# Sparse-and-full causal attention into a max-out FFN: V casts moved off VectorE, the opening reordered

## The chip, the cores and the metric

The kernel runs on one core of a Trainium2 chip. Five engines work side by side, each through its own queue in order: TensorE (matmuls and weight loads), VectorE (DVE in the profile), ScalarE (ACT), GpSimd (POOL) and SyncE (SP, which only issues DMAs here). An instruction that waits holds up all that stands behind it on its engine. The metric is the device time of one execution in microseconds, the median over runs.

## The reference

```python
def _attn_ref(q, k, v, is_retrieval, n_sink, window):      # B, H, S, D = 4, 8, 768, 64
    scores = scale * np.matmul(q, k.transpose(0, 1, 3, 2))
    stream_keep = causal & (is_sink | in_win)              # 4 sinks, a window of 64
    mask = causal if is_retrieval[head] else stream_keep
    a = softmax(where(mask, scores, -1e9))
    return np.matmul(a, v)

def _moe_ref(x, w1, w2, w3, w_out):                        # x: 3072 x 512, w: 512 x 768, w_out: 768 x 512
    h = np.maximum(np.maximum(x @ w1, x @ w2), x @ w3)
    return h @ w_out
```

Attention over 4 batches of 8 heads, where a flag of each head chooses between a full causal mask and a mask of sinks and a window; its result, heads side by side, goes through an FFN with a maximum over three products. All inputs are float32, the work is done in float16 with float32 accumulation.

## The kernel before

A *step* t is a batch, a half of its 768 queries, and four of its eight heads (`where`, L105): steps 0 to 3 are batch 0 (first half: 0 and 1, second half: 2 and 3), steps 4 to 7 batch 1, and so on to 15. The two head pairs of a step are i = 0 and 1. The scores of a step are cut into units u (`UNITS`, L19): two for a first half, four for a second one. For a unit, `scores` (L404) runs matmuls into PSUM (L439), ScalarE takes exp into an SBUF tile `pt` (L450), and `masks` (L460) multiplies blocks of `pt` by the head's mask (L477), on GpSimd unless the triple (t, i, u) stands in `MASK_ON_DVE`. For steps 0 and 1 the mask is added by matmuls instead (L423), so the scores need the mask tiles of `head_masks` (L291), which need the heads' flags (`head_flags`, L274).

`av` (L481) multiplies `pt` by V; V lies in two float16 copies, `va` for blocks near the diagonal and `vf`, multiplied by the head's flag, for far ones. `prep_v` (L384) makes both for a step and a head pair: a cast of the float32 load (L390) on the engine of its first letter, the product (L392) on that of its second. VectorE then takes a reciprocal and a product into x (L501, L503). x is transposed by a DMA, or by TensorE with an eviction (`turn_x`, L518) in steps 0, 1 and 3.

K and Q must stand transposed: in batch 0 they are loaded as float32, cast (`cast_pair`, L133), transposed on TensorE (L155) and evicted (L160, `turn_pair`); in batches 1 to 3 a casting DMA from GpSimd's queue (`load`, L169) is followed by four VectorE transposes for a step's heads (`turn`, L180: K or Q, first or second part). `stage` keeps three buffers of each load.

The FFN of a batch's half is a generator (`ffn`, L317) that yields 24 times: 18 groups of four 384-wide matmuls (L336) and three output blocks. A group of w1 is copied out by ScalarE (L344), those of w2 and w3 are combined by VectorE (L347). All single-bank PSUM tiles, those of FFN groups, V products and transposes, come from one pool of four banks (`bkp`); scores have two tiles of their own. `fill(n)` takes n yields off the queue of FFNs; an FFN enters this queue with `turn_x` of the last pair of its half.

The order is written out by hand: first an opening, line by line (L537 to L592), then `PROGRAM` (L600), one row for each score unit from step 2 on. I call a row a slot: slots 1 to 4 are step 2, 5 to 8 step 3, 9 and 10 step 4, 11 and 12 step 5. A row is (units of FFN to spend, whether the two pairs' scores stand apart, four strings of work: before the scores, after them, after half of the FFN units, after the rest). In the strings `v 2 0 dd` is `prep_v(2, 0)` with VectorE for both parts (a is ScalarE, p GpSimd), and `cast`, `pair`, `turn`, `load`, `load_v`, `av` and `x` name the functions above. `gate` lets SyncE's queue wait for step 3's first exps, so that its later V loads don't take part in the first loads.

The first weight w0 is loaded by `load_weight(0)` (L555) from GpSimd's queue, and so are the K and Q of batch 0's second half (`load_pairs(1, ...)`), the other weights, V of the second half, and all of `load`. `idle_work` (L223) runs matmuls of zeros, to no use but activity.

Of the kernel before, what the change touches and what calls it, by code (L numbers as in the profile page):

```python
# [33 lines left out]
MASKED = [  # L34
    [(0, 0, 1, (0,), 256, 256), (0, 0, 1, (384,), 128, 0), (1, 1, 1, (0,), 256, 0)],
    [(1, 0, 2, (384,), 128, 0), (2, 2, 1, (0, 384), 128, 128), (3, 3, 1, (0,), 256, 0)],
]


def _where(half):  # L40
# [9 lines left out]
def kernel(  # L50
# [14 lines left out]
    nc = tc.nc  # L65
# [50 lines left out]
    cast = {}  # L116
# [200 lines left out]
    def ffn(b, half):  # L317
# [10 lines left out]
        hT = [htp.tile([P, HALF], FP16, tag=f"hT{n}", name=f"hT{n}") for n in range(NNB)]  # L328
        acc = {}
        order = [(wi, ni) for ni in range(NNB) for wi in range(3)]  # L330
        if (b, half) == (0, 0):
            order.sort()
        for wi, ni in order:
            yy = psum()
# [120 lines left out]
                masks(t, i, u)  # L455


    MASK_ON_DVE = ((3, 1, 3), (6, 0, 1), (7, 0, 1))

    def masks(t, i, u):  # L460
        b, half, qd = where(t)
        pt = pts[t, i]
        h0 = 4 * qd + 2 * i
        for at, u0, nu, cols, n, m0 in MASKED[half]:
            if at != u:
                continue
            m = mk[:, h0 : h0 + 2, m0 : m0 + n]
            if nu == 1 and len(cols) == 1:
                x = pt[:, u0, :, cols[0] : cols[0] + n]
            elif nu == 2:  # L470
                x = pt[:, u0 : u0 + 2, :, cols[0] : cols[0] + n]
                m = m.unsqueeze(1).to_broadcast([P, 2, 2, n])
            else:
                x = pt[:, u0].rearrange("p h (c n) -> p h c n", n=n)[:, :, 0:4:3]
                m = m.unsqueeze(2).to_broadcast([P, 2, 2, n])
            engine = nc.vector if (t, i, u) in MASK_ON_DVE else nc.gpsimd
            engine.tensor_tensor(out=x, in0=x, in1=m, op=ALU.mult)  # L477
# [40 lines left out]
    def turn_x(t, i, op=None):  # L518
# [15 lines left out]


    dve, act, pool = nc.vector.tensor_copy, nc.scalar.copy, nc.gpsimd.tensor_copy
    idle_work(8)  # L537
    cast_pair(0, 0, (act, act))
    read_flags()
    head_flags()  # L540
    head_masks(0, True)
    turn_pair(0, 0, dve, dve)
    idle_work(2)
    cast_pair(0, 1, (pool, act))
    head_masks(1, True)
    turn_pair(0, 1, dve)
    cast_pair(0, 2, (pool, pool))
    scores(0, 0, (0,))
    turn_pair(0, 2, dve)
    scores(0, 0, (1,))  # L550
    head_masks(2, True)
    head_masks(3, True)
    cast_pair(0, 3, (pool, pool))
    scores(0, 1, (0,))
    load_weight(0)  # L555
    turn_pair(0, 3, dve)
    far_flags()
    prep_v(0, 0, dve, nc.gpsimd)
    scores(0, 1, (1,))
    prep_v(0, 1, dve, nc.vector)  # L560
    prep_v(1, 0, dve, nc.vector)
    scores(1, 0, (0,))
    scores(1, 1, (0,))
    prep_v(1, 1, dve, nc.gpsimd)
    load_pairs(1, 0, 2, (nc.gpsimd, nc.gpsimd))
    scores(1, 0, (1,))
    scores(1, 1, (1,))
    av(0, 0)
    load_weight(1)
    av(0, 1)  # L570
    load_pairs(1, 2, 2, (nc.gpsimd, nc.gpsimd))
    av(1, 0)
    turn_x(0, 0, act)
    turn_x(0, 1, act)
    av(1, 1)
    turn_x(1, 0, act)
    load_weight(2)
    load_v(0, 1, (nc.gpsimd,) * HB)
    load_weight(3)
    turn_x(1, 1, dve)  # L580
    cast_pair(1, 0, (dve, act))
    cast_pair(1, 1, (dve, act))
    fill(4)
    turn_pair(1, 0, dve)
    turn_pair(1, 1, dve)
    head_masks(0)
    head_masks(1)
    fill(1)
    head_masks(2)
    fill(1)  # L590
    fill(1)
    head_masks(3)  # L592

# [2 lines left out]

    FIRST = 4
    PROGRAM = (  # L600
        (2.4, True, "", "", "cast 1 2 dd", "cast 1 3 ap"),
        (2.4, False, "load 1 0", "", "", ""),
        (2.0, False, "pair 1 2", "", "", "pair 1 3"),
        (2.2, False, "load 1 1", "", "", ""),
        (2.2, True, "", "", "v 2 0 dd", "gate"),
        (1.6, True, "v 2 1 ap, load_v 1 0", "", "av 2 0", ""),
        (1.6, True, "", "x 2 0, turn 1 0 0 0, turn 1 0 0 1", "av 2 1, turn 1 0 1 1", "v 3 0 pp"),
        (3.0, False, "turn 1 0 1 0, load_v 1 1", "x 2 1", "", "v 3 1 ap"),
        (3.6, False, "", "turn 1 1 0 0, turn 1 1 0 1, turn 1 1 1 1, av 3 0", "", "v 4 0 pd"),
        (3.0, False, "av 3 1", "", "", "turn 1 1 1 0, v 4 1 ad"),  # L610
        (3.6, False, "x 3 0, x 3 1", "", "av 4 0", ""),
        (3.6, False, "", "v 5 0 ad, x 4 0, av 4 1", "", "v 5 1 ap, load 2 0"),
        (2.8, False, "", "x 4 1", "", ""),
        (3.6, False, "av 5 0, av 5 1, load 2 1", "x 5 0", "", ""),
        (3.8, False, "v 6 0 pp", "x 5 1", "", "load_v 2 0"),
        (3.4, False, "", "v 6 1 dp", "", "turn 2 0 1 0"),
        (4.8, False, "", "turn 2 0 0 1", "av 6 0", "turn 2 0 0 0"),
        (4.0, False, "", "", "x 6 0, turn 2 0 1 1", "x 6 1"),
        (3.4, False, "", "av 6 1", "turn 2 1 0 0, turn 2 1 0 1", "load_v 2 1"),
        (5.0, False, "", "v 7 0 dp", "turn 2 1 1 0, turn 2 1 1 1", ""),  # L620
        (4.0, False, "v 7 1 dp", "", "", "v 8 0 ap"),
        (3.6, False, "av 7 0, x 7 0, av 7 1", "", "", "v 8 1 dp"),
        (4.0, False, "", "v 9 0 dp", "av 8 0, x 7 1", ""),
        (4.0, False, "", "av 8 1", "x 8 0", "load 3 0"),
        (4.0, False, "", "x 8 1", "av 9 0, v 9 1 dp", ""),
        (4.0, False, "load 3 1", "", "x 9 0", ""),
        (4.2, False, "v 10 0 dp, av 9 1", "", "x 9 1", "load_v 3 0"),
        (4.0, False, "v 10 1 dp", "", "", "turn 3 0 1 0"),
        (4.0, False, "", "turn 3 0 0 1, av 10 0", "", "x 10 0, turn 3 0 0 0"),
        (4.0, False, "", "", "av 10 1, turn 3 0 1 1", ""),  # L630
        (4.4, False, "", "x 10 1", "turn 3 1 0 0, turn 3 1 0 1", "v 11 0 dp, load_v 3 1"),
        (3.2, False, "", "", "turn 3 1 1 0, turn 3 1 1 1", "v 11 1 dp"),
        (4.0, False, "", "", "av 11 0", "v 12 0 dp"),
        (4.2, False, "x 11 0, av 11 1", "", "", "v 12 1 dp"),
        (4.8, False, "", "v 13 0 dp, x 11 1", "av 12 0", ""),
        (4.0, False, "", "av 12 1", "x 12 0", ""),
        (3.2, False, "", "x 12 1", "av 13 0, v 13 1 dp", ""),
        (4.0, False, "", "", "x 13 0", ""),
        (4.0, False, "v 14 0 dp, av 13 1", "", "x 13 1", ""),
        (4.0, False, "v 14 1 dp", "", "", ""),  # L640
        (4.0, False, "", "av 14 0", "", "x 14 0"),
        (4.0, False, "", "", "av 14 1", ""),
        (4.0, False, "", "x 14 1", "", "v 15 0 pp"),
        (4.2, False, "", "", "", "v 15 1 dp"),
        (4.0, False, "", "", "av 15 0", ""),
        (4.0, False, "x 15 0, av 15 1", "", "", ""),
        (4.0, False, "", "x 15 1", "", ""),
    )
    ops = {"d": dve, "a": act, "p": pool}
    engines = {"d": nc.vector, "p": nc.gpsimd}  # L650
# [74 lines left out]
```

## Time and profile before

| | |
|---|---|
| median of 10 runs | 203.73 us (202.21 to 205.49) |
| the profiled execution | 204.06 us, span 202.0 us |
| TensorE busy | 191.4 us (95%) |
| VectorE busy | 130.2 us (64%) |
| ScalarE busy | 124.8 us (62%) |
| GpSimd busy | 125.8 us (62%) |
| V casts (L390) | VectorE 22, mean 636 ns; ScalarE 6, mean 522 ns; GpSimd 4, mean 530 ns |
| mask products (L477) | GpSimd 81, VectorE 3 |
| HBM read, written | 25.17 MB, 6.29 MB |

The span goes from the first to the last instruction of one profiled execution; the time of an execution has some 2 us more. Busy time is an average over stages that differ: what counts in a stage is the wait that ends last. Matmuls are pipelined and their ends are modelled, so busy TensorE isn't TensorE at its peak. In a row of a view, the bracket behind an instruction tells how long its engine stood idle before it and who ended that.

### The profile page before, as it was taken

How to read it: one execution, taken by the hardware profiler on the slowest of the kernel's cores; microseconds unless marked ns; L12 is line 12 of the kernel's file. 1: busy time of each engine (PE TensorE's matmuls, PEld its weight loads, DVE VectorE, ACT ScalarE, POOL GpSimd, SP SyncE). 2: the span in 40 equal slices, each digit the busy share in tenths (PEclk: the TensorE clock that was granted, in tenths of full speed). 3: DMA queues.
4: the chain of work that ended last, by engine and by line, in shares of the span. 5: the costliest groups of instructions: out<-in, count | busy, mean ns of one | idle time of the engine just before them, and what ended most of it. 6: DMA issues, size and time to landing. Idle time of an engine off the chain costs nothing.

```text
span 202.0 us, 5148 instructions
## 1 busy us (share of the span) xinstructions
PE 191.4 (95%) x2059; PEld 109.3 (54%) x2059; DVE 130.2 (64%) x260; ACT 124.8 (62%) x188; POOL 125.8 (62%) x151
## 2 busy tenths in 40 slices
PE   7897899996999999999999999999999999999992
PEld 2555455544556456565556466574565565655652
DVE  2996697889456757985565748986647244633540
ACT  4492797895477778565758596656586776323221
POOL 3669279789993933859987806798929636700000
PEclk9999999999699999999999999999999999999998
DMA  6999999998929991632449982713301230024004
GB/s 181 268 150 236 274 236 206 214 232 187 206 48 191 185 248 59 127 51 76 144 80 204 178 199 83 143 21 124 93 19 24 86 93 19 3 42 153 3 0 156
DMA packets 43245, 26.48 MB, mean 131 GB/s; under 512 B 33558, under 2 KB 38230, under 8 KB 43222
## 3 DMA queue, kind: packets, MB, share of 16 engines
q1 hardware_dynamic: 37206, 15.01, 32.3%
q0 software_dynamic: 4784, 10.23, 26.1%
q10 hardware_dynamic: 1232, 0.92, 1.4%
q8 instruction: 16, 0.26, 0.5%
q14 instruction: 7, 0.06, 0.1%
HBM read 25.17 MB, written 6.29 MB: 156 GB/s over the span
## 4 chain that ended last, share of the span: by engine, by line
PE 82%; DVE 8%; DMA 4%; ACT 3%; POOL 1%; issue 1%; DVEq 0%; ACTq 0%
PE yy L336 43%; PE yy L362 13%; PE st L439 10%; PE oacc L493 9%; PE yst L336 3%; DMA qs<-in_q_dram 3%; DVE KQ L188 2%; PE st L226 2%; DVE KQ L160 2%; DVE mk L293 1%; ACT pt L450 1%; DMA out_dram<-ot 1%; PE tr L155 1%; PE yst L362 1%; ACT ot L368 1%
## 5 line engine op out<-in xcount | busy, mean ns | idle before, releaser
L477 POOL TENSOR_TENSOR pt<-pt,mk 128x512 f16<-128x512 f16 (+1 forms) x81 | 86.6, 1093 | 32.5 <-ACT pt L450 32.4
L450 ACT ACTIVATE pt<-st 128x1024 f16<-128x1024 f32 (+3 forms) x99 | 83.1, 894 | 27.0 <-PE st L439 26.4
L347 DVE TENSOR_TENSOR acc<-yy,acc 128x384 f16<-128x384 f32 x45 | 25.0, 557 | 25.7 <-PE yy L336 17.7
L336 PE MATMUL yy<-xT,w0t 128*128 128x384 f16 x180 | 36.7, 330 | 0.1
L336 PE MATMUL yy<-xT,w1t 128*128 128x384 f16 x180 | 36.7, 328 | 0.0
L336 PE MATMUL yy<-xT,w2t 128*128 128x384 f16 x180 | 36.2, 327 | 0.0
L344 ACT CAST acc<-yy 128x384 f16<-128x384 f32 x45 | 21.3, 481 | 19.9 <-PE yy L336 14.9
L362 PE MATMUL yy<-woutt,hT 128*128 128x512 f16 (+1 forms) x138 | 32.3, 375 | 0.0
L439 PE MATMUL st<-KQ 32*128 32x384 f16 (+5 forms) x560 | 29.2, 283 | 1.1 <-DVE KQ L188 0.7
L347 DVE TENSOR_TENSOR hT<-yy,acc 128x384 f16<-128x384 f32 x45 | 25.1, 557 | 6.4 <-PE yy L336 3.2
L493 PEld LDWEIGHTS <-pt 128*128 128x128 f16 x672 | 24.1, 98 | 5.5 <-issue 1.5
L493 PE MATMUL oacc<-va,pt 128*128 128x65 f16 x352 | 24.9, 194 | 0.8 <-POOL pt L477 0.8
L188 DVE STREAM_TRANSPOSE KQ<-kq 128x384 f32<-128x384 f32 x24 | 25.2, 1137 | 0.2 <-DMA kq<-in_k_dram 0.2
L336 PEld LDWEIGHTS <-w0t 128*128 128x128 f16 x192 | 17.9, 98 | 12.5 <-issue 1.4
L336 PEld LDWEIGHTS <-w2t 128*128 128x128 f16 x192 | 17.7, 98 | 13.0 <-issue 1.9
L336 PEld LDWEIGHTS <-w1t 128*128 128x128 f16 x192 | 17.5, 98 | 12.5 <-issue 1.1
L439 PEld LDWEIGHTS <-KQ 32*128 32x128 f16 (+1 forms) x560 | 12.5, 94 | 19.6 <-issue 13.9
L368 ACT COPY ot<-yy 128x512 f32<-128x512 f32 x22 | 12.9, 588 | 14.8 <-PE yy L362 10.6
L362 PEld LDWEIGHTS <-hT 128*128 128x128 f16 x150 | 13.8, 98 | 15.1 <-DVE hT L347 1.0
L493 PE MATMUL oacc<-vf,pt 128*128 128x65 f16 x320 | 21.4, 193 | 0.2 <-DVE vf L392 0.2
L501 DVE RECIPROCAL rc<-oacc 128x6 f32<-128x6 f32 x32 | 6.2, 193 | 19.6 <-PE oacc L493 19.4
L503 DVE TENSOR_TENSOR x<-oacc,rc 128x384 f16<-128x384 f32 x32 | 17.8, 557 | 1.1
(71 smaller groups left out, 125.6 us busy)
## 6 DMA issues: line engine op xcount, KB each, us to landing
out_dram<-ot SPq DMA_DIRECT2D x23, 256.0 KB, 2.6
vs<-in_v_dram SPq DMA_DIRECT2D x21, 256.0 KB, 5.2
kq<-in_k_dram POOLq DMA_DIRECT2D x6, 384.0 KB, 8.0
kq<-in_q_dram POOLq DMA_DIRECT2D x6, 384.0 KB, 9.4
qs<-in_q_dram ACTq DMA_DIRECT2D x4, 192.0 KB, 4.2
ks<-in_k_dram SPq DMA_DIRECT2D x4, 192.0 KB, 4.0
w0t<-in_moe_w_dram POOLq DMA_DIRECT2D x1, 768.0 KB, 7.0
ks<-in_k_dram POOLq DMA_DIRECT2D x2, 384.0 KB, 7.1
```

The lines of the kernel that those rows point to most:

```text
L188: nc.vector.transpose(out=dst.rearrange("c (p j) -> c j p", j=n)[:, j0:j1], in_=src.rearrange("c (j i) -> c j i", i=R),)
L336: nc.tensor.matmul(yy[:, 0:HALF], w_t[wi][:, ks, ni * P : (ni + 1) * P], xT[b, half][ks].rearrange("p a t -> p (a t)"), start=(ks == 0), s ...
L344: nc.scalar.copy(out=acc[ni], in_=yy[:, 0:HALF])
L347: nc.vector.tensor_tensor(out=dst, in0=yy[:, 0:HALF], in1=acc[ni], op=ALU.max)
L362: nc.tensor.matmul(yo[:, 0:n], hT[ns][:, tb * P : (tb + 1) * P], woutt[:, ns, c : c + n], start=(ns == 0), stop=(ns == NNB - 1),)
L368: op(out=ot[:, c : c + n], in_=yo[:, 0:n])
L439: nc.tensor.matmul(sts[g // m][:, g % m, c0 : c0 + n * P], KQ[rows, 0, ki * P : (ki + 1) * P], KQ[rows, 1, t0 : t0 + n * P], start=(c0 == ...
L450: nc.scalar.activation(out=pts[t, i][:, u, h0 : h0 + m, 0:w], in_=st[:, :, 0:w], func=AF.Exp, scale=sc,)
L477: engine.tensor_tensor(out=x, in0=x, in1=m, op=ALU.mult)
L493: nc.tensor.matmul(o[:, qi, hl, 0 : D + 1], pt[:, u, hl, c : c + P], vv[:, 2 * hp + hl, ki, 0 : D + 1], start=(idx == 0), stop=(idx == len ...
L501: nc.vector.reciprocal(out=rc, in_=o[:, :, :, D])
L503: nc.vector.tensor_tensor(out=x, in0=o[:, :, :, 0:D], in1=rc.unsqueeze(3).to_broadcast([P, HB, 2, D]), op=ALU.mult,)
```

## The change

V casts of steps 2 to 15 are written with `a` or `p` in place of `d`: 21 on ScalarE, 7 on GpSimd, none on VectorE. In steps 0 and 1 one V cast goes to ScalarE, one to GpSimd. Three `vf` products (steps 4 and 5) go from VectorE to GpSimd. Seven more mask products stand on VectorE, where step 3's joint mask of two units is split in two (`APART`). In the opening the first Q is evicted by ScalarE, two filler matmuls are moved ahead of the flags, `load_weight(0)` ahead of the casts of the fourth pair, `load_pairs(1, 0, ...)` ahead of a V step, and all four casts of batch 0's first two second-half pairs are put on ScalarE. The FFN of batch 0's second half also takes its groups in the order of the weights. `PROGRAM` has the same 47 rows, with other units (166.58 in place of 169.8 in all) and places. Of its rows, those up to slot 14 are shown, and slots 20, 27 and 39 of the new one.

```diff
--- before.py
+++ after.py
@@ -35,6 +35,8 @@
     [(0, 0, 1, (0,), 256, 256), (0, 0, 1, (384,), 128, 0), (1, 1, 1, (0,), 256, 0)],
     [(1, 0, 2, (384,), 128, 0), (2, 2, 1, (0, 384), 128, 128), (3, 3, 1, (0,), 256, 0)],
 ]
+
+APART = [(0, 0, 1, (384,), 128, 0), (1, 1, 1, (384,), 128, 0)] + MASKED[1][1:]
 
 
 def _where(half):
@@ -328,7 +330,7 @@
         hT = [htp.tile([P, HALF], FP16, tag=f"hT{n}", name=f"hT{n}") for n in range(NNB)]
         acc = {}
         order = [(wi, ni) for ni in range(NNB) for wi in range(3)]
-        if (b, half) == (0, 0):
+        if b == 0:
             order.sort()
         for wi, ni in order:
             yy = psum()
@@ -455,13 +457,13 @@
                 masks(t, i, u)
 
 
-    MASK_ON_DVE = ((3, 1, 3), (6, 0, 1), (7, 0, 1))
+    MASK_ON_DVE = ((2, 0, 1), (3, 0, 0), (3, 0, 1), (3, 1, 3), (5, 0, 0), (5, 1, 0), (5, 1, 1), (7, 0, 1))
 
     def masks(t, i, u):
         b, half, qd = where(t)
         pt = pts[t, i]
         h0 = 4 * qd + 2 * i
-        for at, u0, nu, cols, n, m0 in MASKED[half]:
+        for at, u0, nu, cols, n, m0 in APART if t in (3,) else MASKED[half]:
             if at != u:
                 continue
             m = mk[:, h0 : h0 + 2, m0 : m0 + n]
@@ -534,62 +536,62 @@
 
 
     dve, act, pool = nc.vector.tensor_copy, nc.scalar.copy, nc.gpsimd.tensor_copy
+    cast_pair(0, 0, (act, act))
     idle_work(8)
-    cast_pair(0, 0, (act, act))
     read_flags()
+    idle_work(2)
     head_flags()
+    turn_pair(0, 0, dve, act)
     head_masks(0, True)
-    turn_pair(0, 0, dve, dve)
-    idle_work(2)
     cast_pair(0, 1, (pool, act))
-    head_masks(1, True)
     turn_pair(0, 1, dve)
     cast_pair(0, 2, (pool, pool))
     scores(0, 0, (0,))
+    scores(0, 1, (0,))
+    head_masks(1, True)
+    load_weight(0)
+    scores(0, 0, (1,))
+    far_flags()
+    cast_pair(0, 3, (pool, pool))
+    head_masks(3, True)
+    head_masks(2, True)
     turn_pair(0, 2, dve)
-    scores(0, 0, (1,))
-    head_masks(2, True)
-    head_masks(3, True)
-    cast_pair(0, 3, (pool, pool))
-    scores(0, 1, (0,))
-    load_weight(0)
+    scores(0, 1, (1,))
     turn_pair(0, 3, dve)
-    far_flags()
     prep_v(0, 0, dve, nc.gpsimd)
-    scores(0, 1, (1,))
-    prep_v(0, 1, dve, nc.vector)
     prep_v(1, 0, dve, nc.vector)
+    load_pairs(1, 0, 2, (nc.gpsimd, nc.gpsimd))
+    prep_v(1, 1, pool, nc.gpsimd)
     scores(1, 0, (0,))
     scores(1, 1, (0,))
-    prep_v(1, 1, dve, nc.gpsimd)
-    load_pairs(1, 0, 2, (nc.gpsimd, nc.gpsimd))
     scores(1, 0, (1,))
+    prep_v(0, 1, act, nc.vector)
+    av(0, 0)
     scores(1, 1, (1,))
-    av(0, 0)
+    av(1, 0)
+    av(0, 1)
+    turn_x(0, 0, act)
+    av(1, 1)
     load_weight(1)
-    av(0, 1)
+    turn_x(0, 1, act)
+    head_masks(0)
+    cast_pair(1, 1, (act, act))
     load_pairs(1, 2, 2, (nc.gpsimd, nc.gpsimd))
-    av(1, 0)
-    turn_x(0, 0, act)
-    turn_x(0, 1, act)
-    av(1, 1)
-    turn_x(1, 0, act)
     load_weight(2)
     load_v(0, 1, (nc.gpsimd,) * HB)
+    turn_x(1, 0, dve)
+    turn_x(1, 1, dve)
+    cast_pair(1, 0, (act, act))
+    fill(4)
+    head_masks(2)
+    turn_pair(1, 1, dve)
+    turn_pair(1, 0, dve)
+    head_masks(3)
     load_weight(3)
-    turn_x(1, 1, dve)
-    cast_pair(1, 0, (dve, act))
-    cast_pair(1, 1, (dve, act))
-    fill(4)
-    turn_pair(1, 0, dve)
-    turn_pair(1, 1, dve)
-    head_masks(0)
-    head_masks(1)
-    fill(1)
-    head_masks(2)
     fill(1)
     fill(1)
-    head_masks(3)
+    fill(1)
+    head_masks(1)
 
 
 
@@ -598,53 +600,53 @@
 
     FIRST = 4
     PROGRAM = (
-        (2.4, True, "", "", "cast 1 2 dd", "cast 1 3 ap"),
-        (2.4, False, "load 1 0", "", "", ""),
-        (2.0, False, "pair 1 2", "", "", "pair 1 3"),
-        (2.2, False, "load 1 1", "", "", ""),
-        (2.2, True, "", "", "v 2 0 dd", "gate"),
-        (1.6, True, "v 2 1 ap, load_v 1 0", "", "av 2 0", ""),
-        (1.6, True, "", "x 2 0, turn 1 0 0 0, turn 1 0 0 1", "av 2 1, turn 1 0 1 1", "v 3 0 pp"),
-        (3.0, False, "turn 1 0 1 0, load_v 1 1", "x 2 1", "", "v 3 1 ap"),
-        (3.6, False, "", "turn 1 1 0 0, turn 1 1 0 1, turn 1 1 1 1, av 3 0", "", "v 4 0 pd"),
-        (3.0, False, "av 3 1", "", "", "turn 1 1 1 0, v 4 1 ad"),
-        (3.6, False, "x 3 0, x 3 1", "", "av 4 0", ""),
-        (3.6, False, "", "v 5 0 ad, x 4 0, av 4 1", "", "v 5 1 ap, load 2 0"),
-        (2.8, False, "", "x 4 1", "", ""),
-        (3.6, False, "av 5 0, av 5 1, load 2 1", "x 5 0", "", ""),
...
+        (2.4, True, "", "", "cast 1 2 dp", ""),
+        (2.4, False, "load 1 0", "", "cast 1 3 da", ""),
+        (2.0, False, "", "pair 1 2", "load 1 1", ""),
+        (2.2, False, "pair 1 3", "v 2 0 ad", "", "v 2 1 ap"),
+        (2.2, False, "", "gate, load_v 1 0", "", ""),
+        (1.6, True, "", "av 2 0", "", "turn 1 0 0 0"),
+        (1.0, True, "turn 1 0 0 1", "", "av 2 1, turn 1 0 1 0", ""),
+        (2.2, True, "turn 1 0 1 1, load_v 1 1", "", "v 3 1 pp, v 3 0 ap, x 2 0", "turn 1 1 0 0"),
+        (3.6, False, "turn 1 1 0 1", "x 2 1", "turn 1 1 1 1, av 3 1", ""),
+        (2.8, False, "v 4 0 pp, av 3 0", "turn 1 1 1 0", "v 4 1 ap", ""),
+        (3.6, False, "x 3 0, x 3 1", "", "", ""),
+        (3.6, False, "av 4 0", "", "x 4 0, v 5 1 pp", "x 4 1, v 5 0 ap"),
+        (2.8, False, "", "", "av 4 1", "av 5 0, load 2 0, v 6 0 pp"),
+        (3.6, False, "x 5 0", "load 2 1", "", "av 5 1"),
...
+        (5.4, False, "load_v 2 1", "v 7 0 ap, turn 2 1 0 0", "turn 2 1 1 0", "v 7 1 ap"),
...
+        (5.6, False, "v 10 0 ap, av 9 1", "v 10 1 ap", "", ""),
...
+        (3.94, False, "v 14 0 ap, av 13 1", "v 14 1 ap", "", ""),
...
     )
     ops = {"d": dve, "a": act, "p": pool}
     engines = {"d": nc.vector, "p": nc.gpsimd}
```

## The prediction, before the change was run

> **What bounds the kernel now.** I read the page first, then the windows, then the chain of waits, then the DMA view.
>
> ```profile
> PE 191.4 (95%) x2059; PEld 109.3 (54%) x2059; DVE 130.2 (64%) x260; ACT 124.8 (62%) x188; POOL 125.8 (62%) x151
> ...
> 46.99:50.40 3.41, 1.93 (x44) 1.25 (x40) 3.32 (x8) 1.49 (x4) 3.41 (x5) 1.00 0.73 195
> 50.40:53.82 3.42, 3.40 (x34) 1.96 (x35) 0.85 (x5) 2.26 (x3) 3.42 (x4) 0.50 1.15 225
> 58.00:182.00 124.00, 123.87 (x1424) 71.21 (x1423) 79.06 (x148) 81.15 (x117) 81.20 (x90) 1.00 0.49 103
> ```
>
> TensorE (first pair of numbers behind each window's length) is busy 123.87 of 124 us between 58 and 182 us: there is nothing to win there, only to lose. So the end is set by when TensorE gets its work in the first 55 us. There the chain runs through other engines:
>
> ```profile
> 14.49 5.58 DMA qs<-in_q_dram
> 20.15 0.92 ACT qn L137 x2
> 21.07 0.39 ACT acc L344
> ...
> 44.30 0.57 DVE pt L477
> 44.88 2.95 DVE KQ L188 x3
> ...
> 47.88 0.56 DVE x L503
> 48.44 0.20 DVE vf L392
> 48.63 0.12 DVE rc L501
> 48.75 0.02 issue
> 48.78 0.56 DVE x L503
> 49.33 1.04 DVE KQ L188
> 50.38 0.05 issue
> 50.42 1.04 PE st L439 x11
> ```
>
> From 44.30 to 50.42 VectorE alone carries the chain: the FFN of batch 0's first half has run dry, the next one needs x of step 3, and the scores of step 5 need the last transpose of K and Q. These transposes in turn hang on the DMA:
>
> ```profile
> GB/s 219 218 153 41 111 206 209 213 187 179 334 289 208 209 209 254 365 339 233 204 204 211 334 230 217 202 208 201 207 217 219 211 209 216 209 209 210 202 256 267
> ...
> q0 software_dynamic: 3632, 7.08, 94.2%
> ...
> 9.35 0.98 POOL L305 DMA_DIRECT2D w0t<-in_moe_w_dram  x1
> ...
> 39.12 2.08 DVE L188 STREAM_TRANSPOSE KQ<-kq 128x384 f32<-128x384 f32 x2 [0.25 <-DMA kq<-in_k_dram]
> ```
>
> The first two lines are the DMA view of 8 to 45 us in slices of 0.925 us, the others the timeline of GpSimd and of VectorE. GpSimd's queue keeps the DMA engines 94.2% busy; only the fourth slice (10.8 to 11.7 us) is nearly empty, 41 GB/s, before the first weight's data start. Everything on that queue lands one behind the other, and VectorE's first transpose at 39.12 waited for its K. A load started earlier moves all that follow.
>
> **The change, part by part.**
>
> *Filler and first eviction.* Two filler matmuls move ahead of the flags. The eight take 3.59 us, 0.43 each with their start, so flags come 0.85 later, near 5.7. VectorE then evicts K (0.54) before building two masks (0.86): ready near 7.5. ScalarE's eviction of Q (0.48, by the same shape at L529) comes before its cast of the second pair's Q (0.51), and TensorE wants that one before the first scores: ScalarE is done near 7.4, three transposes, mask matmuls and scores follow. The first exp starts near 8.45, where the timeline now has 7.69. Cost 0.75 us, at the head of ScalarE's exps.
>
> *The first weight's issue.* GpSimd now casts K and Q of the fourth pair, 8.45 to 9.35, before it issues w0; in the change it issues w0 first. So w0 goes out 0.9 us earlier, into the empty slice. As the queue is full from there on, w1, w2, w_out and batch 1's K and Q land about 0.9 earlier (K of step 4: 38.2). What pays: the fourth pair's casts, behind w0's issue (0.98) and two column copies (0.89), are some 2 us later, so its scores are too. The K and Q loads for the second half go out near 12.1 instead of 13.68, as they pass a V product of step 1 on GpSimd's queue and the masks no longer hold up the columns; w1 and those behind it keep their place or gain about half a microsecond at issue, enough to keep the queue full.
>
> *Steps 0 and 1, x, start of the FFN.* Exps of both steps take 6.3 us on ScalarE (1.02 + 1.57 + 3.75 in the timeline from 7.69 to 15.08); begun at 8.45, with about 1.1 of waiting for the late fourth pair and with the one V cast now put among them (0.51), the last ends near 16.4. x of step 1 follows on VectorE (0.76 each), then two mask builds (0.6) that now stand before the last two evictions: x complete near 19.3 instead of 18.3. This does not reach the path: today ScalarE sits in front of L344 until Q has landed at 20.07 and been cast, and TensorE, four groups in, has no free PSUM bank until 21.5. After, Q lands near 19.1, ScalarE's four casts (4 x 0.51, two of them taken from VectorE) end at 20.6, and TensorE arrives at 19.3 + 0.16 + 3 x 0.65 = 21.4. Of the cover 0.1 us is left: anything later than this costs in full. Slot 1 then starts at 24.4, today 24.46: nothing won, nothing lost.
>
> *Slots 1 to 8.* V of step 2 is cast by ScalarE one slot and a half earlier; the chain's VectorE cast and product before the first output matmul (0.75 + 0.57, of which TensorE waits about 0.45) go. Behind that cast on ScalarE's queue stand the exps of step 3; V lands near 32.4, ScalarE gets there near 33.0, so I cost the wait at nothing, half a microsecond if V is late. `turn 1 0 0 0` now stands in VectorE's queue before the x of step 2's second pair: if K is late, that x waits too. With K at 38.2 and TensorE at slot 7 near 38.5, it isn't.
>
> *Slots 8 to 11, VectorE.* From K's landing VectorE has eight transposes (1.04 each), three times 0.76 for x, a mask and 0.6 of evictions: 11.7 us without a gap, so from 38.2 to 49.9. Today it has the same and two vf products (0.28 and 0.33), one before the last x and one before the eviction. The FFN starts at 51.4 today; after, at 50.0 to 50.2. That is 0.9 from the DMA and about 0.4 from the products: **1.3 us**. GpSimd's side holds: four masks of 1.17 less by then, but it mostly waits for exps anyway; av 3 1 goes first, since GpSimd prepares its V first.
>
> *FFN order of (0,1).* Six ScalarE copies in a row (2.9) meet exps (1.94 + 1.08) and two casts in slots 11 and 12: 6.9 us against TensorE's 6.0. Four banks of 0.65 hide 2.6 us, so 0; up to 0.5 if they don't.
>
> *V casts from slot 12 on.* All in all ScalarE takes 15 more V casts of steps 2 to 15 (6 to 21), GpSimd 3 more (4 to 7), VectorE 18 fewer. Here the row is:
>
> ```profile
> L390 DVE CAST va<-vs x22: 326/484/1333, 12.0 to 174.2; 128x384 f16<-128x384 f32 x22
> L390 ACT CAST va<-vs x6: 512/514/545, 36.0 to 89.6; 128x384 f16<-128x384 f32 x6
> ```
>
> (min, median and max in ns). The Trainium skill, Perfetto Trace Analysis, Optimizing Scalar/DVE Operations, speaks against this: where VectorE has a fast mode it is the quicker engine, and offloading pays if it is saturated. By that the change swaps 0.35 for 0.51 on an engine that isn't saturated, +2.4 us of busy time for 15 casts, and nothing back. The row agrees for a cast that runs alone, but the mean is 0.636 and the worst 1.333, beside GpSimd's products. I go by the row: VectorE loses 18 x 0.64 = 11.5 us, ScalarE gains 15 x 0.51 = 7.7, of 124.8. What that costs TensorE the trace doesn't show; bounds: -0.7 (today's few late maxima go) to +3.0 (0.2 us exposed at each of the 15). In a half of eight slots ScalarE would have about 23 us of work in 29, so I take 0.
>
> *Masks.* Seven more instructions on VectorE (3 to 10, two masks being split), +2.6 us; about -5.8 on GpSimd. They hide where TensorE is the bound: 0.
>
> *The dip.* The windows above show the clock at 0.50 from 50.40 to 53.82, after 3.41 us in which TensorE had 1.93 busy; it costs 1.7 us. The skill's TensorE: Matmul & The Clock Gate, Part 1, has the clock halve after an idle window of about 3.4 us. By that rule alone a window more than half busy shouldn't have done it and any rearrangement could shake it off (-1.7). By the row a half-filled window is enough, and after the change TensorE still has only about 1.5 us of work between 47.0 and 50.4. I keep the dip, and -1.7 for the range.
>
> **Sum.** The profiled execution took 204.06 (span 202.0 and 2.06 around it), 0.33 above the median of 203.73. 204.06 - 1.3 = 202.76; against the median, **202.4 us**. A difference of 0.5%, 1.0 us, is about what a measurement of this kernel tells from none.
>
> **Rivals.** *ScalarE turns into the bound* (slower). Its price: 0.2 us for each of 15 casts, 3.0 - 1.3 = +1.7, 205.4. It decides once a cast next to a slot's two exps (1.94) and another cast keeps L344 waiting beyond four banks, 2.6 us; two casts stand together in slots 20, 27 and 39. For it: ScalarE becomes the busiest after TensorE. Against: ScalarE has 81 of 124 us busy now and waited 26.4 us for scores.
> *The gain is given back* (no change): the opening is later than 19.3 by 0.5 to 1, since the fourth pair's casts and the masks share time; TensorE's lateness reaches x of step 2 and so the transposes. 203.5.
> *The dip goes as well*: 202.4 - 1.7 = 200.7.
> That the casts don't move is excluded: the program's letters set the engine.
>
> **How the numbers follow.** Main case 0.43, dip gone too 0.15, given back 0.25, ScalarE 0.17. The main case is just beyond 0.5% (1.3 us), the second well; so faster 0.58, same 0.25, slower 0.17. The range runs from 200.2 (dip gone, half a microsecond better) to 205.0 (most of the ScalarE case).
>
> **What would show it.** Right: w0 issued near 8.4, first kq transpose near 38.2, the first FFN matmul after slot 11's scores near 50.0, no TensorE gap beyond today's after 58. Wrong: that first transpose at 39 or later (the DMA did not move), TensorE reaching slot 1 after 25 (the opening), L344 waiting at ScalarE and idle TensorE in slots 20 to 40 (ScalarE), the clock at 1.00 throughout (the dip).

## The result, and the profile after

The changed kernel takes 202.11 us (median; 201.42 to 202.88), the kernel before 203.69 (202.21 to 205.79): a ratio of 0.9922, with a 95% interval of 0.9897 to 0.9948. The forecast was 202.4. The profiled execution took 202.01 us, with a span of 200.1. One thing is needed to read the times: in 46 of the 127 executions of the kernel before that stand beside the experiments the mean granted clock was below 0.993 and the time 1.5 to 1.6 us longer (a dip like that at 50.40 us in its profile), in none of the 14 of the changed kernel, and "at full clock" below means without the executions that have such a dip.

The lines of the changed kernel that answer to those shown of before, first from the page and from the windows:

```profile
PE 189.2 (95%) x2059; PEld 109.3 (55%) x2059; DVE 123.4 (62%) x242; ACT 131.6 (66%) x206; POOL 122.5 (61%) x153
```

```profile
46.99:50.40 3.41, 2.22 (x61) 1.71 (x61) 3.32 (x8) 1.76 (x4) 3.41 (x5) 1.00 0.79 190
50.40:53.82 3.42, 3.42 (x41) 2.06 (x42) 2.02 (x4) 2.72 (x5) 3.42 (x6) 1.00 1.10 260
58.00:182.00 124.00, 123.90 (x1418) 72.00 (x1415) 70.46 (x134) 85.00 (x129) 80.85 (x91) 1.00 0.54 107
```

ScalarE has taken over 3.9 us and VectorE lost 8.6 in the stage from 58 us on, and TensorE is as full as it was. The clock is whole where it was halved. The chain of waits still ends on VectorE in slots 9 to 11:

```profile
44.43 0.58 DVE pt L479
45.01 2.95 DVE KQ L190 x3
48.02 0.56 DVE x L505
48.57 0.11 DVE rc L503
48.71 0.56 DVE x L505
49.27 1.06 DVE KQ L190
50.37 0.63 PE st L441 x16
```

The vf product is out of the chain, but its end has hardly moved: 50.37 for 50.42. What became of the DMA's lead is seen in the DMA view from 8 to 45 us, the timeline of GpSimd and that of VectorE:

```profile
GB/s 218 218 203 174 211 186 244 382 337 196 209 196 209 292 369 316 226 214 211 231 330 225 217 190 211 210 201 218 215 215 218 206 216 209 210 214 264 191 228 177
```

```profile
7.97 0.94 POOL L307 DMA_DIRECT2D w0t<-in_moe_w_dram  x1
```

```profile
39.17 2.08 DVE L190 STREAM_TRANSPOSE KQ<-kq 128x384 f32<-128x384 f32 x2
```

The fourth slice is filled (174 for 41 GB/s), w0 goes out 1.4 us earlier, and K of step 4 lands at 37.23 (39.10 before). Yet the first transpose starts at 39.17 and no DMA is named in front of it: VectorE came late by itself. The largest loss of time lies in slot 5 (timeline of all engines, TensorE's weight loads left out):

```profile
32.80 2.29 POOL L479 TENSOR_TENSOR pt<-pt,mk 128x512 f16<-128x512 f16 x2
32.83 2.68 DVE L394 TENSOR_TENSOR vf<-va,far 128x384 f16<-128x384 f16 x1 [1.10 <-ACT va L392]
...
35.44 1.47 DVE L349 TENSOR_TENSOR hT<-yy,acc 128x384 f16<-128x384 f32 x3
...
36.03 0.81 PE L338 MATMUL yy<-xT,w2t 128*128 128x384 f16 x4 [1.67 <-DVE hT L349]
```

The vf product of `v 2 0`, 0.56 us in the kernel before, takes 2.68 beside two mask products of GpSimd. Both of its inputs lie in SBUF, as GpSimd's do. Three evictions stand behind it in VectorE's queue, and TensorE waits 1.67 us for them.

The intervals between slots 1 and 13 repeat to within 0.05 us where the same code runs (but for e8, and where the clock dips); the opening does not (slot 1 moves by over a microsecond between executions of one kernel). So I compare intervals between the first score matmuls of slots:

| us from slot to slot | start to 1 | 1–5 | 5–9 | 9–11 | 11–13 | 13 to end |
|---|---|---|---|---|---|---|
| before, second profile (clock whole) | 25.53 | 9.27 | 10.26 | 6.43 | 6.67 | 143.65 |
| after | 23.73 | 9.27 | 11.66 | 5.71 | 6.04 | 143.71 |
| e2: before, new opening | 24.60 | 9.27 | 10.26 | 6.44 | 6.67 | 143.65 |
| e7: after, old opening | 25.08 | 9.26 | 11.66 | 5.70 | 6.04 | 143.68 |
| e8: before, w0 first (a dip) | 25.67 | 9.27 | 10.53 | 6.17 | 8.05 | 143.66 |
| e3: before, casts alone (a dip) | 24.73 | 9.26 | 10.51 | 7.63 | 7.81 | 143.39 |
| e1: after, `v 2 0` on GpSimd | 24.13 | 9.26 | 10.58 | 5.51 | 6.04 | 143.71 |
| e5: e1, step 3's masks back | 24.00 | 9.27 | 10.21 | 5.69 | 6.04 | 143.70 |
| g3: e5, old FFN order | 23.18 | 9.27 | 10.22 | 5.71 | 6.85 | 143.71 |
| g4: e5, step 5's masks back | 24.07 | 9.26 | 10.23 | 5.70 | 6.03 | 147.25 |

The change wins in the opening, loses 1.40 in slots 5 to 9, wins 0.72 and 0.63 in the next two and is neutral afterwards. My theory at this point: the opening is the gain, the program nets zero, and the vf product in slot 5 is what it lost. The rivals: the casts are the gain; the missing dip is.

### The profile page after: what moved, and what is told of

Read it like the earlier page. It is cut to its first block, busy times and chain, and to the rows that moved or that the text cites. A ratio compares the mean times of both kernels' runs of the same rounds, so it can differ in the third digit from the quotient of the medians.

```text
span 200.1 us, 5133 instructions
## 1 busy us (share of the span) xinstructions
PE 189.2 (95%) x2059; PEld 109.3 (55%) x2059; DVE 123.4 (62%) x242; ACT 131.6 (66%) x206; POOL 122.5 (61%) x153
## 3 DMA queue, kind: packets, MB, share of 16 engines
q0 software_dynamic: 4784, 10.23, 26.7%
HBM read 25.17 MB, written 6.29 MB: 157 GB/s over the span
## 4 chain that ended last, share of the span: by engine, by line
PE 74%; DMA 10%; POOL 6%; DVE 3%; issue 2%; ACT 2%; SPq 1%; DVEq 0%; ACTq 0%; POOLq 0%
PE yy L338 39%; PE yy L364 13%; PE st L441 9%; PE oacc L495 9%; DMA vs<-in_v_dram 6%; PE yst L338 3%; DMA ks<-in_k_dram 2%; DVE KQ L190 2%; ACT pt L452 1%; DMA out_dram<-ot 1%; POOL vs L208 1%; POOL qs L126 1%; POOL ks L126 1%; PE yst L364 1%; ACT ot L370 1%
## 5 line engine op out<-in xcount | busy, mean ns | idle before, releaser
L479 POOL TENSOR_TENSOR pt<-pt,mk 128x512 f16<-128x512 f16 (+1 forms) x76 | 80.4, 1082 | 37.2 <-ACT pt L452 37.2
L338 PE MATMUL yy<-xT,w1t 128*128 128x384 f16 x180 | 36.1, 327 | 0.1
L338 PE MATMUL yy<-xT,w0t 128*128 128x384 f16 x180 | 35.6, 326 | 0.4 <-DVE xT L531 0.4
L441 PE MATMUL st<-KQ 32*128 32x384 f16 (+4 forms) x560 | 28.5, 279 | 0.6 <-DVE KQ L190 0.5
L190 DVE STREAM_TRANSPOSE KQ<-kq 128x384 f32<-128x384 f32 x24 | 25.7, 1131 | 0.0
```

The costliest lines, as they stand in the source:

```text
L190: nc.vector.transpose(out=dst.rearrange("c (p j) -> c j p", j=n)[:, j0:j1], in_=src.rearrange("c (j i) -> c j i", i=R),)
L338: nc.tensor.matmul(yy[:, 0:HALF], w_t[wi][:, ks, ni * P : (ni + 1) * P], xT[b, half][ks].rearrange("p a t -> p (a t)"), start=(ks == 0), s ...
L441: nc.tensor.matmul(sts[g // m][:, g % m, c0 : c0 + n * P], KQ[rows, 0, ki * P : (ki + 1) * P], KQ[rows, 1, t0 : t0 + n * P], start=(c0 == ...
```

## The experiments

**The two halves of the change.** e2 is the kernel before with all lines of the new opening, of which the diff shows those around w0:

```diff
-    cast_pair(0, 3, (pool, pool))
-    scores(0, 1, (0,))
-    load_weight(0)
...
+    load_weight(0)
+    scores(0, 0, (1,))
+    far_flags()
+    cast_pair(0, 3, (pool, pool))
...
```

> The kernel before with the changed kernel's opening (all up to the first program row), its own program, masks and V casts. My theory: the opening gains 0.7 us at slot 1 (23.73 against 24.46), through the first weight's earlier issue; K of step 4 lands near 37.3 instead of 39.1. With the old program it isn't lost in slot 5, so slot 11's scores come 0.7 to 1.5 us earlier than 50.42 and the time is 202.2 to 203.0, less 1.7 where the clock doesn't dip. Rival (the opening is hidden): VectorE's chain from step 3's exps to slot 11 doesn't move, the time is 203.7 within 0.4.

It took 202.48 us, ratio 0.9891 [0.9852, 0.9931]; at full clock 201.79 (four executions) for 203.38. The time is as forecast, its profile is not: slot 1 came at 24.60 and slot 11 at 50.57, and from slot 1 on every interval is that of the kernel before, though K had landed at 37.84. e7 is the other half, the changed kernel with the old opening (the diff is the same, reversed):

> The kernel before's opening with all the rest of the change (program, masks, casts, FFN order). My theory: the opening is what gains (before with the new opening alone was 201.79 in its executions without a dip, against 203.38), the program gives some of it back through the stuck product in slot 5 but keeps the clock up: 203.0 to 203.8, no dips. Rival (the program gains by itself): 202.1 to 202.8.

203.81 us, ratio 1.0009 [0.9978, 1.0040]; at full clock 203.79 for 203.75; 3 of its 14 executions have a dip, where I had expected none. So the whole gain is the opening's, as far as these times tell, and the new program with its casts and masks nets nothing. The table shows what is inside this zero: +1.40, -0.73 and -0.63.

**What of the opening pays.** e8 moves one line of the kernel before:

```diff
+    load_weight(0)
     cast_pair(0, 3, (pool, pool))
     scores(0, 1, (0,))
-    load_weight(0)
```

> The kernel before with one line moved: the first weight's load is issued before the casts of the fourth pair instead of after them. Theory of the prediction: all on GpSimd's queue lands 0.9 us earlier, K of step 4 near 38.2, and most of the opening's gain is this: 0.6 to 1.2 us off the executions without a dip (202.2 to 202.8 against 203.38). Rival (the gain of the opening is the order of scores and x, or ScalarE's evictions): the fourth pair comes 1 us later, the load's lead is lost, 203.4 or more.

203.39 us, ratio 0.9981 [0.9955, 1.0007]; at full clock 202.89 for 203.75, which is 0.86 less. 9 of its 21 executions have a dip, and over all of them the gain is not clear of noise. Its profile, one of the 9, doesn't show the gain: w0 goes out at 8.44, but the second half's Q lands at 20.07 as in the first profile of the kernel before, slot 1 comes at 25.67, and K of step 4 lands at 40.70. g2 takes the same thing out of the new opening, where w0 then goes out at 9.58 us:

```diff
-    load_weight(0)
     scores(0, 0, (1,))
-    far_flags()
     cast_pair(0, 3, (pool, pool))
+    load_weight(0)
+    far_flags()
```

> The kernel before with the new opening, but load_weight(0) and far_flags() left behind the fourth pair's casts as before. My theory: the earlier w0 is most of what the opening gains (0.9 of 1.1 to 1.6 us), so this runs at 202.6 to 203.4 us where the clock is not halved, slot 1 near 25.0 us. Rival: the new order of evictions, scores and products on ScalarE is the gain, and w0 only goes with it: then 201.8 us, like the whole opening.

202.97 us, ratio 0.9982 [0.9956, 1.0008]; at full clock 202.76 for 203.34. The new opening without the early w0 wins 0.6, with it 1.6: the early w0 (with `far_flags` in g2) is worth 0.9 to 1.0 by adding it and by taking it away. The remaining 0.6 belongs to the rest of the new order; I have not split it. The second profile of the kernel before went with it:

> The kernel before again, for a second profile of it. If the half-empty window in slot 11 falls well on the grid, the clock stays at full and the span is near 201.5 us, with slots 11 to 13 taking 6.7 us where the first profile had 7.96; if it halves again, near 203. Slot 1 between 24.4 and 25.1 us, slots 5 to 9 10.2 to 10.3 us, slots 9 to 11 6.4 us: then the differences that I read between single profiles in slots 5 to 11 are of the kernels and those at slot 1 are partly of the execution.

Slot 1 came at 25.53, later than I had allowed, with the clock whole and a span of 201.8. Four profiles with the old opening (without the one of e4, whose clock was halved early) have slot 1 at 24.46, 24.73, 25.08 and 25.53, seven with the new one between 23.18 and 24.63; the means are 24.95 and 24.05 (e8 with 25.67 and g2 with 25.03 are neither). From slot 1 to the end b2, e2 and g2 all take 176.3 us and the changed kernel 176.4: what the opening gains, it gains before slot 1. The waits of TensorE between 16 and 26 us show how two executions differ there, first of the kernel before again, then of the changed kernel:

```profile
PE tr L155 <- ACT acc L344: 1.3, 1, 1.3
PE tr L525 <- DVE x L503: 0.9, 2, 0.6
```

```profile
PE tr L527 <- DVE x L505: 0.5, 2, 0.3
PE yy L338 <- DVE xT L531: 0.4, 1, 0.4
```

The wait for a free bank behind ScalarE's eviction, 0.9 in the first profile and 1.3 here, is gone: the casts of the second half's Q and K end at 20.37, and ScalarE has evicted before TensorE arrives. The new order alone does not take it away, for e2 has the same opening and this among its waits:

```profile
PE tr L155 <- ACT acc L344: 1.3, 1, 1.3
```

There the second half's Q landed at 19.96, in the changed kernel at 18.95. In six profiles (e1, e2, e5, e6, e7, g2) slot 1 comes 4.63 to 4.65 us after this landing, in the others 4.4 to 5.9. Where w0 went out before 8.4 us, Q landed at 18.37 to 19.36 (but 19.96 in e2), where after 9, at 19.90 to 20.56 (but 21.12 in e4). That the early w0 pays by an earlier Q is therefore my reading; no run holds Q's landing fixed.

Of K's landing the profiles tell more. In six of them the order of the kernel before runs from slot 1 on (before, b2, e2, e4 with its filler, e8, g2). K of step 4 lands between 13.24 (e2) and 15.03 us (e8) after slot 1, and slot 11 comes 25.95 to 25.97 us after slot 1 in all six. The timeline of VectorE has the reason, first of the kernel before, then of e2:

```profile
44.30 0.57 DVE L477 TENSOR_TENSOR pt<-pt,mk 128x512 f16<-128x512 f16 x1 [0.49 <-ACT pt L450]
```

```profile
44.44 0.57 DVE L477 TENSOR_TENSOR pt<-pt,mk 128x512 f16<-128x512 f16 x1 [0.55 <-ACT pt L450]
```

After its first four transposes VectorE stands idle until ScalarE gives it step 3's last exp. The chain to slot 11 starts at this exp. The 0.25 us that the first transpose waited for K were covered by the 0.49 of the same engine later on.

**Casts alone.** e3 is the kernel before with other letters for its V casts, 18 fewer of them on VectorE, and nothing else, for example:

```diff
-        (2.2, True, "", "", "v 2 0 dd", "gate"),
+        (2.2, True, "", "", "v 2 0 ad", "gate"),
...
-        (1.6, True, "", "x 2 0, turn 1 0 0 0, turn 1 0 0 1", "av 2 1, turn 1 0 1 1", "v 3 0 pp"),
-        (3.0, False, "turn 1 0 1 0, load_v 1 1", "x 2 1", "", "v 3 1 ap"),
+        (1.6, True, "", "x 2 0, turn 1 0 0 0, turn 1 0 0 1", "av 2 1, turn 1 0 1 1", "v 3 0 ap"),
+        (3.0, False, "turn 1 0 1 0, load_v 1 1", "x 2 1", "", "v 3 1 pp"),
...
-        (4.2, False, "v 10 0 dp, av 9 1", "", "x 9 1", "load_v 3 0"),
+        (4.2, False, "v 10 0 ap, av 9 1", "", "x 9 1", "load_v 3 0"),
```

> The kernel before with nothing but the first letters of its V steps from step 2 on as in the changed kernel (ScalarE 21, GpSimd 7, VectorE none); places, products, opening and masks as before. Theory of the prediction: the casts are hidden in the steady part, and VectorE's work is not on the path there: same as before, 203.7 within 0.5, TensorE busy from 58 to 182 us as before. Rival 1 (VectorE's relief is what the change gains): 202.1 to 202.7. Rival 2 (ScalarE turns late): 204.5 to 206.5, with idle TensorE in slots 16 to 40.

205.83 us, ratio 1.0106 [1.0080, 1.0131]: slower, where I had forecast no change. From slot 13 on, casts off VectorE win 0.26 (143.39 for 143.65), in slots 5 to 9 they cost 0.25. The loss lies in slots 9 to 11, and it does not come of a cast taken off VectorE: with the changed kernel's letters, step 3's first cast goes from GpSimd to ScalarE and its second the other way. The first of them, in the timeline of GpSimd before and of ScalarE in e3:

```profile
43.19 0.50 POOL L390 CAST va<-vs 128x384 f16<-128x384 f32 x1
```

```profile
43.22 0.51 ACT L390 CAST va<-vs 128x384 f16<-128x384 f32 x1
```

In e3 it stands in front of step 3's last exps. From VectorE's timeline there, and the windows for the stretch that follows:

```profile
45.18 0.85 DVE L477 TENSOR_TENSOR pt<-pt,mk 128x512 f16<-128x512 f16 x1 [0.96 <-ACT pt L450]
...
49.52 0.82 DVE L392 TENSOR_TENSOR vf<-vs,far 128x128 f16<-128x128 f32 x1
```

```profile
50.40:53.82 3.42, 2.03 (x22) 0.98 (x23) 2.67 (x6) 0.55 (x1) 3.18 (x4) 0.71 1.14 235
```

Counted from slot 9 (43.99 before, 44.50 here) the mask starts 0.37 later, and it takes 0.85 for 0.57; the vf product takes 0.82 for 0.28. That is 1.19 of the 1.20 us. In the window the clock is 0.71: TensorE ran dry longer, and all 21 executions have at least one dip.

**Casts from step 6 on.** e6 is the changed kernel with all V casts from step 6 on back on VectorE:

```diff
-        (3.2, False, "v 11 1 pp", "x 10 1, turn 3 1 1 1", "v 12 0 ap", "av 11 0, x 11 0"),
+        (3.2, False, "v 11 1 dp", "x 10 1, turn 3 1 1 1", "v 12 0 dp", "av 11 0, x 11 0"),
```

> The changed kernel with the V casts of steps 6 to 15 back on VectorE (16 from ScalarE, 4 from GpSimd), all else as changed. Theory of the prediction: from slot 13 on TensorE is the bound and the engine of these casts is of no account: 202.1 within 0.4. Rival 1 (VectorE's relief pays late): slower, 202.8 to 204. Rival 2 (ScalarE's load costs now): faster, 201 to 201.6.

203.27 us, ratio 0.9982 [0.9961, 1.0004], where the changed kernel has 0.9922: as rival 1 had it. From slot 13 to the end it takes 144.5 for 143.7, and slot 28 alone takes 1.04 more (timeline):

```profile
108.28 3.36 DVE L392 CAST va<-vs 128x384 f16<-128x384 f32 x1
108.36 0.85 POOL L394 TENSOR_TENSOR vf<-va,far 128x384 f16<-128x384 f16 x1
...
109.14 2.27 POOL L479 TENSOR_TENSOR pt<-pt,mk 128x512 f16<-128x512 f16 x2
...
112.16 0.81 PE L338 MATMUL yy<-xT,w2t 128*128 128x384 f16 x4 [0.91 <-DVE acc L349]
```

The cast that takes 0.35 a microsecond earlier takes 3.36, until three GpSimd instructions are through, and TensorE waits 0.91. So in the new order the casts are better off VectorE; in the old one they cost it 0.3 at most.

**The product in slot 5.** e1 changes one letter of the changed kernel:

```diff
-        (2.2, False, "pair 1 3", "v 2 0 ad", "", "v 2 1 ap"),
+        (2.2, False, "pair 1 3", "v 2 0 ap", "", "v 2 1 ap"),
```

> The changed kernel with one letter other: the far copy of V for step 2, first pair, is multiplied by GpSimd instead of VectorE (ad becomes ap). My theory (the port): in the changed kernel this product took 2.68 us on VectorE instead of 0.56, because it ran beside two mask products of GpSimd; two FFN evictions stood behind it and TensorE waited 1.67 us. Then here no such product, no gap in slot 5, TensorE reaches slot 9's scores some 1.5 us earlier than 44.66, and since VectorE's transposes then start near 38 instead of 39.17, the whole is faster than the changed kernel by 1.0 to 1.8 us: 200.3 to 201.1. Rival (the end of the stall is set elsewhere): K and Q land no earlier and the chain from step 3's last exp to slot 11 is as long; the gap goes but slot 11's scores stay near 50.3, and the time is 202.1 within 0.4.

201.03 us, ratio 0.9832 [0.9799, 0.9865], 1.08 below the changed kernel, and slots 5 to 9 take 1.08 less. The wait of 1.67 is gone, and the time lies in the forecast. But the first transpose is no earlier (39.22), for another VectorE instruction has now run into GpSimd's work (timeline):

```profile
33.19 2.29 POOL L479 TENSOR_TENSOR pt<-pt,mk 128x512 f16<-128x512 f16 x2
...
34.88 2.32 DVE L479 TENSOR_TENSOR pt<-pt,mk 128x256 f16<-128x256 f16 x1 [0.83 <-ACT pt L452]
...
35.41 1.62 POOL L394 TENSOR_TENSOR vf<-va,far 128x384 f16<-128x384 f16 x2
```

A mask of half that size, 0.27 us alone, ends at 37.20, after GpSimd's last product. It is one of those that the change brought to VectorE, so e5 puts step 3's two back on GpSimd and drops `APART`:

```diff
-    MASK_ON_DVE = ((2, 0, 1), (3, 0, 0), (3, 0, 1), (3, 1, 3), (5, 0, 0), (5, 1, 0), (5, 1, 1), (7, 0, 1))
+    MASK_ON_DVE = ((2, 0, 1), (3, 1, 3), (5, 0, 0), (5, 1, 0), (5, 1, 1), (7, 0, 1))
...
-        for at, u0, nu, cols, n, m0 in APART if t in (3,) else MASKED[half]:
+        for at, u0, nu, cols, n, m0 in MASKED[half]:
```

> The changed kernel with the far product of step 2's first pair on GpSimd, and with step 3's first mask products of the first pair back on GpSimd, unsplit. Theory (the port): with only the former, a 128x256 mask product on VectorE then took 2.32 us instead of 0.27 beside GpSimd's products, two FFN evictions behind it, and VectorE's first transpose began at 39.22 although K had landed at 37.70. Without it that transpose begins within 0.3 us of K's landing, slot 11's scores come 0.8 to 1.5 us earlier than 49.48, and the time is 199.7 to 200.4 against 201.03. Rival (GpSimd was relieved for good reason): its mask products reach step 3's V product late, TensorE waits for them before av 3 1, and the time is 201.0 to 202.0.

200.76 us (200.42 to 201.25), ratio 0.9858 [0.9827, 0.9889]: the fastest kernel here. That it beats e1 by 0.27 is not settled, as the two ran beside different runs of the kernel before and their intervals overlap; in the profile slots 5 to 9 go from 10.58 to 10.21. The time lies between my forecast and the rival's. Slot 11 came at 49.17, 0.31 earlier where I had 0.8 to 1.5, and VectorE's first transpose 0.75 after K's landing (37.23), behind a product of x:

```profile
37.98 2.08 DVE L190 STREAM_TRANSPOSE KQ<-kq 128x384 f32<-128x384 f32 x2
```

In g3 and g4 below it follows K by 0.23 and 0.10, and slot 11 comes 25.17 to 25.19 us after slot 1 in all three.

**The terms that I put at zero.** Two experiments take the FFN order and step 5's masks out of e5.

```diff
-        if b == 0:
+        if (b, half) == (0, 0):
```

> The best version so far (the after kernel, v 2 0 on GpSimd, step 3's two masks back on GpSimd: 200.76 us) with the old order for the second half's first FFN. My theory: the order is worth nothing to 0.3 us, 200.4 to 201.1 us. Rival: in slots 11 to 13 the new order is what keeps ScalarE or VectorE from holding TensorE up, then 201.3 to 201.8 us and slots 11 to 13 take 6.6 us where they took 6.04.

201.50 us, ratio 0.9882 [0.9846, 0.9918]. The interval overlaps that of e5, but the profile decides for the rival: slots 11 to 13 take 6.85 for 6.04, all else from slot 1 on is equal. The timeline of g3, and then of e5 at the same place:

```profile
50.16 2.50 DVE L479 TENSOR_TENSOR pt<-pt,mk 128x512 f16<-128x512 f16 x4 [1.40 <-ACT pt L452]
...
52.58 0.55 DVE L349 TENSOR_TENSOR acc<-yy,acc 128x384 f16<-128x384 f32 x1
...
53.18 0.81 PE L338 MATMUL yy<-xT,w1t 128*128 128x384 f16 x4 [0.76 <-DVE acc L349]
```

```profile
49.74 2.77 PE L338 MATMUL yy<-xT,w0t 128*128 128x384 f16 x16
...
51.73 1.64 ACT L346 CAST acc<-yy 128x384 f16<-128x384 f32 x4
```

With the old order the second group already needs VectorE, which has four masks in front; with the new one the first six groups need ScalarE alone. Then the masks of step 5:

```diff
-    MASK_ON_DVE = ((2, 0, 1), (3, 1, 3), (5, 0, 0), (5, 1, 0), (5, 1, 1), (7, 0, 1))
+    MASK_ON_DVE = ((2, 0, 1), (3, 1, 3), (7, 0, 1))
```

> The best version so far (200.76 us) with step 5's three masks back on GpSimd. My theory: they are covered either way, 200.4 to 201.1 us. Rival: GpSimd then gives the V products or casts of steps 4 and 5 late, and a slot in 12 to 16 waits for them: 201.3 to 201.8 us. Third: VectorE's masks are held by GpSimd's products as the vf product in slot 5 was, and on GpSimd they are cheaper: 200.0 to 200.4 us.

205.22 us, ratio 1.0058 [1.0030, 1.0085]: slower than the kernel before, and at full clock 204.51, 3.75 above e5 (which ran beside other runs of the kernel before). Of this, 3.3 lies at two places: slot 13 to 14 takes 4.73 for 3.36, slot 17 to 18 6.74 for 4.86. The timeline of GpSimd ahead of the first, and then TensorE's at both:

```profile
52.79 5.74 POOL L479 TENSOR_TENSOR pt<-pt,mk 128x512 f16<-128x512 f16 x6
58.48 0.49 POOL L392 CAST va<-vs 128x384 f16<-128x384 f32 x1
```

```profile
59.74 0.19 PE L495 MATMUL oacc<-vf,pt 128*128 128x65 f16 x1 [1.21 <-POOL vf L394]
...
74.36 0.32 PE L338 MATMUL yy<-xT,w0t 128*128 128x384 f16 x1 [1.73 <-DMA xT<-x]
```

GpSimd's V cast and product come behind six masks, and its load of step 6's K goes out at 59.64, 3.2 us after that of e5 (56.41). The last DMA transpose of x, issued at 64.68 among these loads, is then waited for until 74.36. That the late loads delay the transpose is my reading; no run tried it apart.

**The dip.** e4 puts ten matmuls of zeros into the gaps of slots 9 and 11 of the kernel before, into a bank of its pool:

```diff
-        (3.6, False, "x 3 0, x 3 1", "", "av 4 0", ""),
+        (3.6, False, "x 3 0, idle 3, x 3 1, idle 3", "", "av 4 0", ""),
-        (3.6, False, "", "turn 1 1 0 0, turn 1 1 0 1, turn 1 1 1 1, av 3 0", "", "v 4 0 pd"),
+        (3.6, False, "", "turn 1 1 0 0, turn 1 1 0 1, turn 1 1 1 1, idle 4, av 3 0", "", "v 4 0 pd"),
```

> The kernel before with ten matmuls of zeros in three gaps that TensorE has anyway (four before the first output of step 3, three and three around the transposes of slot 11); no other work moves. Theory (the dip is worth 1.7 us and comes of a half-empty window): the clock stays at 1.00 from 6 us on in every run, the spread of the times shrinks from 3.6 us to some 1.5, and the median is 202.0 to 202.7. Rival (the dip hides behind ScalarE and VectorE, or comes by itself): the clock stays up and the time is 203.7 within 0.4, or it falls again, elsewhere.

203.04 us, ratio 0.9980 [0.9957, 1.0004]; a dip in 1 of 22 executions, where the kernel before has 14 of 42 beside it. The one is the profiled execution, and there the clock is halved at 23.52, in the opening. So the gaps make the dips, and filling them takes them away. But the median gains less than I forecast: a dip costs 1.5 to 1.6 us, but only a third of the executions have one, and the median of the kernel before is 0.20 to 0.22 lower at full clock than over all its executions.

## Why the prediction was right, and where its steps were not

The number holds: 203.69 to 202.11 is 1.58, of which 0.2 is the missing dips and about 1.4 the sum that I had put at 1.3. One cause in it was right, the first weight's earlier issue, worth 0.9 to 1.0. Its path was not, and that the rest comes out is luck: in the program +1.40, -0.72 and -0.63 cancel, and I had foreseen none of the three in this size.

- *Filler and first eviction*, +0.75 at the first exp (8.45 forecast): 8.59 in this execution, though 7.64 in e2 with the same opening. The means of the profiles, 8.23 with the new opening and 7.65 with the old one, give 0.58. That it is hidden no run tried apart.
- *The first weight's issue*, 0.9 earlier: 1.4 in this execution (9.35 to 7.97), 1.1 in the mean of the profiles. K of step 4 landed at 37.23 where I had 38.2.
- *Steps 0 and 1, x, start of the FFN*: "nothing won, nothing lost" failed, and it is here that the gain arises. I had Q landing at 19.1 (it was 18.95) and the casts ending at 20.6 (20.37), but charged the exps' delay to x: complete at 19.3, it was complete at 18.85. So TensorE went on at 21.02 without a wait, where I had it arrive at 21.4. The end of its wait for ScalarE's eviction (0.9 to 1.3) became a gain; I had spent that on a later x. Over the profiles slot 1 comes 0.9 earlier.
- *Slots 1 to 8*: "I cost the wait at nothing" looked at the cast alone. The cast on ScalarE was in time; the product behind it, left on VectorE, met GpSimd's two masks and took 2.68 for 0.56. This term was missing: 1.40 us. And the wait that went was not 0.45 but 0.25.
- *Slots 8 to 11*: "That is 0.9 from the DMA" failed. I let the chain start at K's landing and run without a gap. It starts at step 3's last exp, for which VectorE waited 0.49 in the profile that I had, and slot 11 didn't move against slot 1 when K's landing did (e2, e8). The vf product out of the chain gave 0.18 from the mask to slot 11 (5.94 for 6.12), where I had 0.4 for two products. The other 0.54 of the 0.72 is that the mask comes earlier against slot 9; no run took that apart.
- *FFN order: 0* and *masks: 0* failed as separate terms: taken out of e5, the order is worth 0.8, step 5's masks over 3. I asked what each adds to an engine with time to spare, not what it takes off the engine that the V products were moved to. They make room for the moved products, and the row of busy shares could not show it.
- *V casts from slot 12 on: 0*: right for the sum. By the rule of the Trainium skill that I had named there (Perfetto Trace Analysis, Optimizing Scalar/DVE Operations: the quicker engine unless it is saturated) the move should win nothing. From slot 13 on it won 0.3 at most in the old order (e3) and 0.8 in the new one (e6), where one held-up cast made the difference.
- *The dip kept*: wrong. The window of 46.99 to 50.40 has 2.22 us of TensorE's work where I had 1.5 and before 1.93, and none of the 14 executions has a dip; with the old opening (e7) 3 of 14 have one. It moved the median by 0.2 only, since the kernel before has it in a third of its executions.

Of the rivals, ScalarE as the bound is excluded (123.90 of 124 us of TensorE from 58 on). "The gain is given back" was true within the program, by slot 5, and not for its reason, a late opening.

## To carry to other kernels

An instruction with both inputs in SBUF can take several times its own row on VectorE when GpSimd works beside it (2.68 for 0.56 us here): look at GpSimd's timeline at the place where the change puts it, and at what stands behind it in VectorE's queue. When a change moves work in a ring from one engine to the next, don't put its small moves at zero one by one; ask which of them makes room for which. Before you price an earlier landing, follow the engine that waited for it: a wait costs nothing if the same engine waits longer for something else further down the chain. A gain in the median can be the sum of a larger gain and a loss at another place: split the change at its seams, and the loss may be a letter to mend.

## What the runs showed of the hardware

I had not expected how long VectorE can be held up. The Trainium skill, SBUF — State Buffer, Who interferes with whom, says that VectorE and GpSimd share a port pair as an exclusive lock: a VectorE instruction with two SBUF inputs, or a copy or cast in one of its two-port modes, that meets a GpSimd instruction reading SBUF, issued before it, waits until that one is through. By that, the product of slot 5 would have waited for the first mask, which took 1.19 us; it took 2.68 and ended 0.4 after the second mask. The mask of e1 (0.27 alone, 2.32 there) ended after three GpSimd instructions, the cast of e6 (0.35 alone, 3.36 there) too, though it is recorded as starting 0.08 before the first of them. In these three places GpSimd's instructions stood back to back, and VectorE didn't come in between two of them at the first chance. Elsewhere it did: the mask of e3 at 45.18 ended 0.28 after the one GpSimd instruction that it had met, the product at 49.52 0.15 after. What makes the difference is open.

The clock was halved after windows in which TensorE was far from idle: 1.93 of 3.41 us busy in the kernel before. The same gaps led to a dip in a third of its executions only. In the four profiles with a halved stretch (before, e3, e4, e8) it begins 44.37, 47.79, 17.07 and 47.79 us after the clock had first become whole, which are 13, 14, 5 and 14 times 3.413; the stretch itself lasts 3.41. The windows of this grid just ahead had 1.93, 1.04, 1.56 and 1.89 us of TensorE's work. In b2 the same gap lay across two windows of its grid, the emptier with 2.34, and no dip followed. So where a gap falls on the grid seems to decide, but busy time is not all of it, for a window on the changed kernel's grid with less work was followed by no dip:

```profile
34.07:37.48 3.41, 1.74 (x19) 0.79 (x18) 3.41 (x6) 1.57 (x3) 2.75 (x3) 1.00 1.10 215
```
